# Emitting TensorE's work by the clock of a planner in the builder, in place of a fixed cycle of two steps

## The chip, the core and the metric

The kernel runs on one core of a Trainium2 chip. The metric is device time in microseconds (us). Matrix products run on TensorE (PE in the profile), exponentials on ScalarE (ACT), most copies out of PSUM on VectorE (DVE), a few small operations on GpSimd (POOL); SyncE (SP) issues the DMAs. Each engine executes its own instructions in the order in which the builder, a Python program, emitted them. An instruction that waits holds up all that stand behind it on its engine.

## The reference

Two layers of attention and MLP on 2048 rows of width 512, each with a layer norm ahead and a residual sum. The second pair uses the same weights as the first. 32 heads of width 16 share one key and one value head.

```python
q = (x @ wq).reshape(B, S, H, Dh)            # S = 2048, H = 32, Dh = 16
k = x @ wk
v = x @ wv
scores = jnp.einsum("bhqd,bkd->bhqk", q, k) * (Dh ** -0.5)
p = _softmax(scores, axis=-1)
o = jnp.einsum("bhqk,bkd->bhqd", p, v)       # then @ wo
...
h = jnp.maximum(jnp.einsum("bsd,df->bsf", x, w1), 0)   # Dff = 1792
h @ w2
...
x = x + _A_ref(_layernorm(x, axis=-1), A_wq, A_wk, A_wv, A_wo)
x = x + _B_ref(_layernorm(x, axis=-1), B_w1, B_w2)
x = x + _A_ref(_layernorm(x, axis=-1), A_wq, A_wk, A_wv, A_wo)
x = x + _B_ref(_layernorm(x, axis=-1), B_w1, B_w2)
```

## The kernel before

**Units and steps.** The attention of both layers is cut into 64 units: 2 layers, 4 blocks of 512 query rows, 8 units of four heads. A unit has 16 steps, one for each tile of 128 keys; that makes 1024 steps (`order`). In a step, `scores` (L707, L708) runs twice. Each time, two matmuls, one on each half of the array's rows, fill one PSUM tile of 128x1024 (`fst`; there are two, one for each half step), and ACT takes the exponential of it into half of the SBUF tile `fp` (three buffers). `front` emits the first half step and `back` the second. The text calls such a half step S. `values` (L713) is V: four matmuls of 32 columns side by side, which add the step's values to `facc`. That is one PSUM tile in all; at the end of a unit DVE copies it out (`keep`, L720) before the next unit may begin. A tile `fst` can be written again when its exponential is done, so the S after next waits for ACT.

**Dense work.** Projections, the output product, the MLP, transposes and layer norms of a block are written as Python generators (`start`, `late`, `chain`, `queries`, `keys`), which emit some instructions and then yield how many slots of PE these took. One slot is a unit of dense work, W. In `batch` (L97) two products share the array by rows: two matmuls of 64 rows make one W, and after a turn of mostly 12 W the halves swap. Between the turns DVE reads one element of each result (`fseen`, L125), and behind the second turn the results are taken out of PSUM: for the MLP by L578 and L579, for the sums into the residual by L497. There are three tiles `fmisc` for all that. Where a later step needs a result at once, `until` forces its generator to run to that point; the products are then not paired (L94) and ACT helps to empty PSUM.

**What each layer waits for.** A chain of a block (output product, MLP, in the first layer also the keys of the second, for one block its queries too) is about 390 to 466 W and is due some 130 steps later; `rate` spreads what is left of it over the steps up to its due time. Since the keys of the second layer need the chain of the last block of the first, a long run of forced dense work stands early in the second layer's steps (1398 to 1457 us).

**The order on PE.** `in_pairs` emits two steps at a time. Its cycle is S S, half a window of W, S, the other half, S, then the values of two steps, V V. A window has 6, 8 or 12 W (`FEW`, `MANY`, `MOST`), by how much dense work is due. If less than 6 is due, or after a yield that asks for a pause, it emits S S V S S V with no W. A window ends at a yield of the form `("lag", n)`.

```python
            front(i)
            back(i)
            w, pause = self.window(size / 2)
...
            front(i + 1)
...
                w, pause = self.window(size - w)
...
            back(i + 1)
            products(i - 1, i)
```

**The end of a unit.** `after(i)` follows the V of a step. At the last step of a unit it issues the copy of the sums to DRAM (L729). For each second unit it then calls, by step number, `unit_sums` one step later (a DMA reads the denominators back, `flsum`), `unit_inverse` three steps later (L746 to L748 on DVE, which wait for that DMA) and `unit_norm` six steps later (L760 to L762, which wait for `frinv`, another round trip through DRAM).

Of the kernel before, what the change touches and what calls it, by code (L numbers as in the profile page):

```python
# [31 lines left out]
FEW, MANY, MOST = 6.0, 8.0, 12.0  # L32
# [8 lines left out]
class _Net:  # L41
# [55 lines left out]
    def batch(self, *jobs, between=None):  # L97

        mm = self.nc.tensor.matmul
        if self.exact or self.solo or self.forced or len(jobs) == 1:  # L100
            for ops, empty, rest in jobs:
                ps = self.misc()
                yield from self.mm3(ps, ops)
                empty(ps)
                if between:
                    between()
                    between = None
                yield from rest()
            return
        ps = [self.misc(), self.misc()]  # L110
        n = len(jobs[0][0])
        for turn in range(2):
            for i in range(n):
                for h in range(2):
                    j = h ^ turn
                    a, b = jobs[j][0][i]
                    r = slice(64 * h, 64 * h + 64)
                    mm(ps[j], a[r], b[r], start=(turn == 0 and i == 0), stop=(turn == 1 and i == n - 1),  # L118
                       skip_group_check=True)
                if i < n - 1:  # L120
                    yield 1.0
            if not turn:

                for t in ps:
                    self.nc.vector.tensor_copy(self.wt("seen", [1, 1]), t[0:1, 0:1])  # L125
# [153 lines left out]
    def keys(self, L, b, to=None):  # L279
        nc = self.nc  # L280
        ps = self.misc()
# [8 lines left out]
        yield ("lag", 0)  # L290
# [31 lines left out]
    def queries(self, L, b, groups, to=None):  # L322
# [7 lines left out]
        yield ("lag", 0)  # L330
# [38 lines left out]
    def start(self):  # L369
# [22 lines left out]
        for t in range(KT):  # L392
# [9 lines left out]
            if t % 2:  # L402
                yield ("lag", 0)
# [9 lines left out]
            if t == 3:  # L413
                yield from self.queries(0, 0, [0])
                yield from self.keys(0, b, self.xt2)
            elif t % 4 == 3:
                yield ("lag", 0)
                yield from self.keys(0, b, self.ot2)
                yield from self.queries(0, 0, [b])
# [10 lines left out]
    def late(self, L, blocks):  # L430

        xs = self.residual(L, blocks[0])
        yield ("lag", 1)
        for b in blocks:
            todo = []
            for s in range(4):
                self.ln(xs[s], s, todo)
                if s % 2:
                    yield ("lag", 0)
# [4 lines left out]
            yield ("lag", 0)  # L444
# [73 lines left out]
    def chain(self, L, b):  # L518
# [63 lines left out]
        def up(f):  # L582
# [7 lines left out]
            else:  # L590
                split(f + 2, (0,))

                def between():
# [3 lines left out]
                                     lambda ps, g=g: hidden(g, ps), lambda: ()) for g in (f, f + 1)], between=between)  # L597
# [23 lines left out]
        ready = []  # L621
# [19 lines left out]
    def flip(self, todo):  # L641

        while todo:
            yield from self.transposed(*todo.pop(0))
            yield from self.transposed(*todo.pop(0))
            yield ("lag", 0)
# [121 lines left out]
    def advance(self):  # L768
# [7 lines left out]
        g[1] -= self.worth(w)  # L776
        return w

    def worth(self, w):
        return w if not isinstance(w, tuple) else w[2] if len(w) > 2 else 0.0  # L780
# [28 lines left out]

    def window(self, n):  # L810

        done = 0.0
        while done < n and self.gens:
            w = self.advance()
            done += self.worth(w)
            if isinstance(w, tuple):
                return done, w[1]
        return done, None
# [32 lines left out]
    def in_pairs(self, n, front, back, product, after):  # L851


        due, hold, size = 0.0, 0, None

        def products(*js):
            for j in js:
                product(j)
                after(j)

        front(0)
        back(0)
        for i in range(1, n - 1, 2):
            due = min(due + 2 * self.rate(i, due), 2 * MOST) if self.gens else 0.0
            if hold or not self.gens or due < FEW:
                hold = max(0, hold - 1)
                for j in (i, i + 1):
                    front(j)
                    back(j)
                    products(j - 1)  # L870
                continue
            if size is None:
                size = MOST if due > 2 * MANY else MANY if due > MANY - 1 else FEW
            front(i)
            back(i)
            w, pause = self.window(size / 2)
            due -= w
            if w < 1.0:
                products(i - 1)
                front(i + 1)  # L880
                back(i + 1)
                products(i)
                hold, size = pause or 0, None
                continue
            front(i + 1)
            if pause is None:
                w, pause = self.window(size - w)
                due -= w
            back(i + 1)
            products(i - 1, i)  # L890
            if pause is not None:
                hold, size = pause, None
        front(n - 1)
        back(n - 1)
        products(n - 2, n - 1)

    def run(self):
        self.normed, self.todo = (1, 3), []
        self.have, self.haveq = [0, 0], {(L, b): 0 for L in range(2) for b in range(NB)}
        self.gens, self.lag, self.left, later = [], 0, 0.0, {}  # L900
# [74 lines left out]
        else:  # L975
            self.in_pairs(n, front, back, product, after)
# [85 lines left out]
```

## Time and profile before

| | us |
|---|---|
| runs of the kernel | 2729.46, 2724.5, 2721.78 (median 2724.5) |
| time of the profiled execution | 2722.86 |
| its span | 2721.0 |
| PE busy | 2469.6 (91%) |
| ACT busy | 1985.5 (73%) |
| DVE busy | 726.5 (27%) |
| first value product, last | 41, 2606 |

The profile is of one execution. Its span runs from the first instruction to the last; the execution's own time is 1.9 longer. In a row of the timeline stand the start, the length, the engine, the line, what is written and read, the shape and the number of instructions; behind it, in brackets, the idle time ahead and what ended it. Matmuls overlap, and their ends are modelled: the price of one is read from the distance of the starts. V appears as 8 matmuls for a step, since each of its four is recorded twice. In a view of stretches, x gives the number of instructions in each.

### The profile page before, as it was taken

What the parts mean: (1) busy time and instruction counts of PE and PEld (TensorE: products, weight loads), DVE (VectorE), ACT (ScalarE), POOL (GpSimd) and SP (SyncE); (2) the same over time, 40 slices, a digit from 0 to 9 for tenths busy, and PEclk for the clock granted to TensorE, in tenths of its full rate; (3) what the DMA queues carried; (4) which work ended last, traced back from release to release, by engine and by line L of the source; (5) the groups of instructions that cost most, each with busy time, mean ns of one, the idle gap of its engine ahead of it and who ended that gap; (6) DMA issues with size and microseconds to landing.
All of it is one profiled execution on the core that took longest, in us unless ns stands there. A gap on an engine that the chain in (4) does not pass through costs nothing.

```text
span 2721.0 us, 44845 instructions
## 1 busy us (share of the span) xinstructions
PE 2469.6 (91%) x18981; PEld 805.8 (30%) x18981; DVE 726.5 (27%) x1560; ACT 1985.5 (73%) x2112; POOL 211.5 (8%) x291
## 2 busy tenths in 40 slices
PE   6798888999899999999798988999999999999979
PEld 2222222323233333333243222233323332333324
DVE  4532324323231123111333122221113111311132
ACT  5687886777677788888642988787888887887830
POOL 2221114310000000000000010000000000000000
PEclk8998998999999999999899999999999999999989
DMA  2112123211221102110221121211022110211022
GB/s 83 46 55 75 37 79 116 72 56 39 70 69 54 34 34 71 61 50 26 78 66 35 51 64 42 81 54 58 28 69 69 53 35 21 84 60 54 20 98 71
DMA packets 106309, 157.78 MB, mean 58 GB/s; under 512 B 19425, under 2 KB 39153, under 8 KB 106097
## 3 DMA queue, kind: packets, MB, share of 16 engines
q1 hardware_dynamic: 106096, 154.82, 17.4%
q8 instruction: 150, 2.46, 0.4%
q14 instruction: 63, 0.51, 0.1%
HBM read 108.86 MB, written 45.88 MB: 57 GB/s over the span
## 4 chain that ended last, share of the span: by engine, by line
PE 52%; ACT 20%; DMA 3%; DVE 3%; issue 3%; POOL 1%; SPq 1%; ACTq 0%; POOLq 0%; DVEq 0%
PE facc L713 23%; ACT fp L708 20%; PE fmisc L118 12%; PE fst L707 12%; PE fmisc L94 5%; DMA flsum<-fod 1%; DMA frinv<-frd 1%; DMA frd<-flsum 0%; DMA fod<-faccs 0%; DVE fbst L245 0%; SPq L360 0%; DVE fxt L497 0%; POOL fbmv L249 0%; DVE fxtl L269 0%; POOL fwraw L459 0%
## 5 line engine op out<-in xcount | busy, mean ns | idle before, releaser
L708 ACT ACTIVATE fp<-fst 128x1024 f32<-128x1024 f32 x2048 | 1941.9, 1028 | 527.9 <-PE fst L707 522.0
L713 PE MATMUL facc<-fp,fva 128*32 128x512 f32 x8192 | 1021.3, 606 | 4.6 <-DVE faccs L720 4.3
L707 PE MATMUL fst<-fqop,fkop 64*128 64x512 f16 x4096 | 738.6, 383 | 127.6 <-ACT fp L708 84.7
L707 PEld LDWEIGHTS <-fkop 64*128 64x128 f16 x4096 | 217.0, 94 | 915.2 <-issue 822.7
L713 PEld LDWEIGHTS facc<-fp,fva 128*32 128x32 f32 x8192 | 203.5, 109 | 469.4 <-issue 456.1
L118 PE MATMUL fmisc<-fxth,fw 64*128 64x512 f16 x1408 | 232.7, 379 | 15.0 <-DVE fseen L125 13.7
L118 PE MATMUL fmisc<-fw,fhh 64*128 64x512 f16 x1344 | 216.4, 377 | 7.5 <-DVE fseen L125 7.3
L497 DVE SCALAR_TENSOR_TENSOR fxt<-fmisc,fxt 128x512 f32<-128x512 f32 x156 | 103.2, 684 | 371.6 <-PE fmisc L118 326.7
L125 DVE COPY fseen<-fmisc 1x1 f32<-1x1 f32 x240 | 25.6, 142 | 535.8 <-PE fmisc L118 535.4
L248 POOL TENSOR_SCALAR fbmv<-fbmv 128x1 f32<-128x1 f32 x84 | 22.2, 265 | 1853.3 <-DVE fbmv L247 1851.9
L118 PEld LDWEIGHTS <-fw 64*128 64x128 f16 x2112 | 110.9, 94 | 119.9 <-issue 19.6
L118 PE MATMUL fmisc<-fxtl,fw 64*128 64x512 f16 x704 | 137.8, 378 | 0.0
L118 PE MATMUL fmisc<-fw,fhl 64*128 64x512 f16 x672 | 130.8, 376 | 0.0
L720 DVE COPY faccs<-facc 128x512 f32<-128x512 f32 x64 | 44.1, 690 | 256.9 <-PE facc L713 256.9
L578 DVE TENSOR_SCALAR fhh<-fmisc 128x512 f16<-128x512 f32 x86 | 58.9, 685 | 184.4 <-PE fmisc L118 184.2
L265 PE MATMUL fmisc<-fident,fxn 128*128 128x128 f32 x336 | 57.5, 311 | 49.4 <-DVE fxn L254 45.4
L579 DVE SCALAR_TENSOR_TENSOR fhl<-fmisc,fhh 128x512 f16<-128x512 f32 x112 | 77.3, 691 | 57.3 <-ACT fhh L576 54.3
L118 PEld LDWEIGHTS <-fhh 64*128 64x128 f16 x1344 | 70.4, 94 | 73.3 <-issue 12.9
L576 ACT ACTIVATE fhh<-fmisc 128x512 f16<-128x512 f32 x26 | 15.4, 597 | 96.0 <-PE fmisc L94 92.1
L94 PE MATMUL fmisc<-fw,fhh 128*128 128x512 f16 x224 | 66.6, 379 | 0.0
L265 PEld LDWEIGHTS fmisc<-fident,fxn 128*128 128x128 f32 x336 | 41.0, 156 | 70.5 <-DVE fxn L254 48.0
L94 PE MATMUL fmisc<-fxth,fw 128*128 128x512 f16 x192 | 59.7, 388 | 0.7 <-ACT fxth L87 0.7
(132 smaller groups left out, 1308.8 us busy)
## 6 DMA issues: line engine op xcount, KB each, us to landing
fw<-fwd SPq DMA_DIRECT2D x196, 256.0 KB
fod<-faccs SPq DMA_DIRECT2D x64, 256.0 KB
fqop<-fqd SPq DMA_DIRECT2D x128, 98.0 KB
fxt<-in_A_x_dram SPq DMA_DIRECT2D x44, 256.0 KB
fqd<-fqh SPq DMA_DIRECT2D x128, 64.0 KB
foraw<-fod SPq DMA_DIRECT2D x32, 256.0 KB
frinv<-frd SPq DMA_DIRECT2D x32, 256.0 KB
fwraw<-in_B_w_dram SPq DMA_DIRECT2D x28, 256.0 KB
```

The source lines that it names most:

```text
L94: self.nc.tensor.matmul(ps, a, b, start=(i == 0), stop=(i == n - 1))
L118: mm(ps[j], a[r], b[r], start=(turn == 0 and i == 0), stop=(turn == 1 and i == n - 1), skip_group_check=True)
L125: self.nc.vector.tensor_copy(self.wt("seen", [1, 1]), t[0:1, 0:1])
L248: nc.gpsimd.tensor_scalar(mv[:, 2:3], mv[:, 1:2], EPS, self.xs ** -2, op0=ADD, op1=MUL)
L265: nc.tensor.transpose(ps[:, c * P:(c + 1) * P], xn[:, c * P:(c + 1) * P], self.ident)
L497: self.nc.vector.scalar_tensor_tensor(xt, ps, 1.0 / factor, xt, op0=MUL, op1=ADD)
L578: nc.vector.tensor_scalar(hh, ps, 0.0, None, op0=MAX)
L579: nc.vector.scalar_tensor_tensor(hl, ps, 0.0, _f(hh), op0=MAX, op1=SUB)
L707: nc.tensor.matmul(st[:, hf], self.kop[U // 32][h, kt * P:(kt + 1) * P], q[h, pr, :], start=True, stop=True)
L708: nc.scalar.activation(p[:, 2 * pr:2 * pr + 2], st, AF.Exp, scale=self.up ** -2)
L713: self.nc.tensor.matmul(acc[32 * j:32 * j + 32], self.va[U // 32][:, kt], p[:, 2 * pr + hf], start=start, stop=stop, skip_group_check=True)
L720: self.nc.vector.tensor_copy(self.sums[U], acc)
```

## The change

`in_pairs` and `window` go, and `timed` takes their place. It keeps a clock of its own: `now` for PE and `act` for ACT. S, V, W and the exponential have fixed costs in it, so have the change from S or W to V (`ENTER`) and back (`LEAVE`), and the delays between the engines. Whenever PE is free by this clock, it picks the next piece: S if its PSUM tile is free by then, V if its exponentials are done, W if dense work is due and no pause is running. V waits until it fits, or until three steps' values stand together (the three buffers of `fp` set that limit). So the values of one to three steps follow each other. Each yield of the generators now also tells a pause, `free`, in the same clock: it is the time for which no further W is emitted, 0.5 to 3.6. The numbers of exponentials, products and DMAs are the same; 36 W are emitted unpaired that were paired.

```diff
-FEW, MANY, MOST = 6.0, 8.0, 12.0
+SCORE, VALUE, DENSE, EXP = 0.216, 0.858, 0.2155, 0.925
+TO_ACT, TO_PE, ENTER, LEAVE, COPY = 0.2, 0.22, 0.126, 0.116, 1.1
+PRESSED, FORCED, FULL = 6.0, 12.0, 14.0
...
-    def batch(self, *jobs, between=None):
+    def batch(self, *jobs, between=None, hold=1.0):
...
-                yield 1.0
+                yield ("lag", 0, 1.0, 0.5)
...
-        yield ("lag", 0, 1.0)
+        yield ("lag", 0, 1.0, hold)
...
-            yield from self.batch(*jobs[i:i + 2])
+            yield from self.batch(*jobs[i:i + 2], hold=1.6)
...
-                    yield ("lag", 0)
+                    yield ("lag", 1, 0.0, 3.6)
...
+        while len(done) < n:
+            k, j = len(exps), len(done)
+            step = k // 2
+            ready = exps[k - 2] + TO_PE if k > 1 else 0.0
+            if k == 2 * n or (step > 2 and j <= step - 3):
+                ready = 1e9
+            made = max(exps[2 * j + 1] + 0.1, sums) if 2 * j + 1 < k else 1e9
+            work = bool(self.gens) and due >= 1.0 and now >= free
+            gap = ready - now
+            if last == "product" and made <= now and due >= PRESSED:
+                kind = "product"
+            elif gap <= (LEAVE if last == "product" else 0.0) and not (work and due >= FORCED):
+                kind = "score"
+            elif made <= now + ENTER and gap >= 0.8 and not (work and due >= PRESSED and last != "product" and step - j < 2):
+                kind = "product"
+            elif work:
+                kind = "work"
+            elif made <= now + 0.2 and gap >= 0.6:
+                kind = "product"
+            else:
+                kind = "score" if ready < 1e9 else "product"
+            turn(kind)
...
+                act = max(act, now + TO_ACT, done[step - 3] + TO_ACT if step > 2 else 0.0) + EXP
+                exps.append(act)
+            elif kind == "work":
+                w = self.advance()
+                now += DENSE * self.worth(w)
+                due -= self.worth(w)
+                if isinstance(w, tuple):
+                    free = now + w[3]
+            else:
+                now = max(now, made if made < 1e9 else 0.0) + VALUE
+                product(j)
+                after(j)
+                done.append(now)
+                sums = now + COPY if j + 1 < n and self.first(j + 1) else 0.0
```

What moves shows first on PE in the second layer, around step 846. Before, the order there is a run of two V, then four score matmuls (`fst`, S S), then dense work (`fmisc`):

```order
L713 MATMUL facc<-fp,fva_78 32x512 x8
L707 LDWEIGHTS fkop_76
L707 MATMUL fst_20340<-fqop_91,fkop_76 128x512
L707 LDWEIGHTS fkop_76
L707 MATMUL fst_20340<-fqop_91,fkop_76 128x512
L707 LDWEIGHTS fkop_76
L707 MATMUL fst_20344<-fqop_91,fkop_76 128x512
L707 LDWEIGHTS fkop_76
L707 MATMUL fst_20344<-fqop_91,fkop_76 128x512
L118 LDWEIGHTS fhl
L118 MATMUL fmisc<-fw_19456,fhl 128x512
```

Now a single V (4 matmuls) stands there, one S behind it, and one or two W before the next S:

```order
L716 MATMUL facc<-fp,fva_78 32x512 x4
L710 LDWEIGHTS fkop_76
L710 MATMUL fst_20230<-fqop_90,fkop_76 128x512
L710 LDWEIGHTS fkop_76
L710 MATMUL fst_20230<-fqop_90,fkop_76 128x512
L122 LDWEIGHTS fw_19907
L122 MATMUL fmisc<-fxtl,fw_19907 128x512
L122 LDWEIGHTS fw_19903
L122 MATMUL fmisc<-fxtl,fw_19903 128x512
L710 LDWEIGHTS fkop_76
L710 MATMUL fst_20236<-fqop_90,fkop_76 128x512
L710 LDWEIGHTS fkop_76
```

V has moved between the two S of a step, and W with it. A little further in the changed order, where much dense work is due, stands a run of three V:

```order
L716 MATMUL facc<-fp,fva_78 32x512 x12
L710 LDWEIGHTS fkop_76
L710 MATMUL fst_20325<-fqop_91,fkop_76 128x512
L710 LDWEIGHTS fkop_76
L710 MATMUL fst_20325<-fqop_91,fkop_76 128x512
L710 LDWEIGHTS fkop_76
L710 MATMUL fst_20329<-fqop_91,fkop_76 128x512
L710 LDWEIGHTS fkop_76
L710 MATMUL fst_20329<-fqop_91,fkop_76 128x512
L122 LDWEIGHTS fhh
L122 MATMUL fmisc<-fw_19434,fhh 128x512
```

Behind it two S follow at once as before; the six W after them come without a break. In all, the order before has 627 runs of V (397 of two, 230 of one), the changed one 693 (501 of one, 53 of two, 139 of three).

On DVE the second place is the end of a unit in the second layer (unit 45). `faccs` is the copy of the unit's sums, `fgood` and the two rows after it are `unit_inverse`. Before:

```order
L720 COPY faccs<-facc 128x512
L125 COPY fseen<-fmisc 1x1 x2
L578 TENSOR_SCALAR fhh<-fmisc 128x512
L579 SCALAR_TENSOR_TENSOR fhl<-fmisc,fhh 128x512
L578 TENSOR_SCALAR fhh<-fmisc 128x512
L579 SCALAR_TENSOR_TENSOR fhl<-fmisc,fhh 128x512
L746 SCALAR_TENSOR_TENSOR fgood<-flsum,fgood 128x32 x2
L747 TENSOR_SCALAR flsum<-flsum 128x32
L748 RECIPROCAL flsum<-flsum 128x32
L760 TENSOR_TENSOR foraw<-foraw,frinv 128x512
```

And in the changed order:

```order
L723 COPY faccs<-facc 128x512
L129 COPY fseen<-fmisc 1x1 x2
L749 SCALAR_TENSOR_TENSOR fgood<-flsum,fgood 128x32 x2
L750 TENSOR_SCALAR flsum<-flsum 128x32
L751 RECIPROCAL flsum<-flsum 128x32
L763 TENSOR_TENSOR foraw<-foraw,frinv 128x512
L764 CAST foth<-foraw 128x512
L765 TENSOR_TENSOR fotl<-foraw,foth 128x512
```

The four evictions of an MLP batch (`fhh`, `fhl`) stood ahead of `fgood`; they now come later, and `fgood` follows the copy and one pair of `fseen`.

More of the change, by code (lines that the diff above doesn't have):

```diff
@@ L289, in keys @@
             eng.tensor_sub(kop[r:r + DH], kv[r:r + DH], _f(kop[r:r + DH]))
-        yield ("lag", 0)
+        yield ("lag", 0, 0.0, 1.2)
         ps = self.misc()
@@ L326, in queries @@
         for i in range(0, len(jobs), 2):
-            yield from self.batch(*jobs[i:i + 2])
+            yield from self.batch(*jobs[i:i + 2], hold=1.6)
         if self.exact:
             return
-        yield ("lag", 0)
+        yield ("lag", 1, 0.0, 2.4)
         ps = self.misc()
@@ L401, in start @@
             yield from self.transposed(xn[t], t % 4, self.ot2 if b else self.xt2)
-            if t % 2:
-                yield ("lag", 0)
+            yield ("lag", 0, 0.0, 2.4)
             if t == 1:
@@ L416, in start @@
             elif t % 4 == 3:
-                yield ("lag", 0)
+                yield ("lag", 0, 0.0, 1.6)
                 yield from self.keys(0, b, self.ot2)
@@ L432, in late @@
         xs = self.residual(L, blocks[0])
-        yield ("lag", 1)
+        yield ("lag", 1, 0.0, 2.0)
         for b in blocks:
@@ L438, in late @@
                 if s % 2:
-                    yield ("lag", 0)
+                    yield ("lag", 1, 0.0, 3.6)
                     yield from self.transposed(*todo.pop(0))
@@ L443, in late @@
                 xs = self.residual(L, b + 1)
-            yield ("lag", 0)
+            yield ("lag", 0, 0.0, 3.0)
             yield from self.queries(L, b, range(4))
@@ L596, in up @@
             yield from self.batch(*[(self.projection(w[0, g], slice(0, P), self.xt2),
-                                     lambda ps, g=g: hidden(g, ps), lambda: ()) for g in (f, f + 1)], between=between)
+                                     lambda ps, g=g: hidden(g, ps), lambda: ()) for g in (f, f + 1)], between=between, hold=1.6)
         def down(fs):
@@ L645, in flip @@
             yield from self.transposed(*todo.pop(0))
-            yield ("lag", 0)
+            yield ("lag", 1, 0.0, 3.2)
     def finish(self, L, b, s, xt, apart):
@@ L776, in advance @@
         g[1] -= self.worth(w)
+        self.spent += self.worth(w)
         return w
     def worth(self, w):
-        return w if not isinstance(w, tuple) else w[2] if len(w) > 2 else 0.0
+        return w[2] if isinstance(w, tuple) else w
     def until(self, done):
@@ L808, in pump @@
         return 0.0
[L810 to L818, printed above, removed]
     def order(self):
@@ L849, in alternate, with timed, turn @@
                     back(i + 1)
[L851 to L857, printed above, removed]
+    def timed(self, steps, front, back, product, after):
+        n = len(steps)
+        now = act = due = free = sums = 0.0
+        exps, done, last = [], [], None
+        def turn(kind):
+            nonlocal now, last
+            if (kind == "product") != (last == "product"):
+                now += ENTER if kind == "product" else LEAVE
+            last = kind
+        while len(done) < n:
[20 more added lines that the diff above has]
+            turn(kind)
+            if kind == "score":
+                now = max(now, ready) + SCORE
+                if k % 2 == 0:
+                    before = self.spent
+                    front(step)
+                    now += DENSE * (self.spent - before)
+                    due = min(due + self.rate(step, due), FULL) if self.gens else 0.0
+                else:
+                    back(step)
+                act = max(act, now + TO_ACT, done[step - 3] + TO_ACT if step > 2 else 0.0) + EXP
[6 more added lines that the diff above has]
+                    free = now + w[3]
+            else:
+                now = max(now, made if made < 1e9 else 0.0) + VALUE
@@ L858, in products @@
                 product(j)
                 after(j)
[L861 to L892, printed above, removed]
@@ L893, in in_pairs @@
-        front(n - 1)
-        back(n - 1)
-        products(n - 2, n - 1)
+                done.append(now)
+                sums = now + COPY if j + 1 < n and self.first(j + 1) else 0.0
     def run(self):
@@ L975, in run @@
         else:
-            self.in_pairs(n, front, back, product, after)
+            self.timed(steps, front, back, product, after)
         while not self.exact and self.gens:
```

2 lines of the change are left out of this document (1 added, 1 removed).

## The prediction

> **What bounds the kernel now.** I read the page first, then the budget by stretches, then one piece of the timeline on PE and ACT, and last the list of waits. The profiled execution took 2722.9 us by its own time, 1.9 more than its span, and lies 1.6 under the median of the three runs (2724.5); the sum below is made against 2722.9.
>
> ```profile
> span 2721.0 us, 44845 instructions
> PE 2469.6 (91%) x18981; PEld 805.8 (30%) x18981; DVE 726.5 (27%) x1560; ACT 1985.5 (73%) x2112; POOL 211.5 (8%) x291
> ```
>
> PE is busy for 91% of the span and ACT for 73%. Neither is full, and both are needed by each of the 1024 steps. A step has two pairs of score matmuls (S), two exponentials on ACT, and one value product (V). Between them stand units of dense work (W: one slot of the MLP or of a projection).
>
> ```profile
> L708 ACT ACTIVATE fp<-fst 128x1024 f32<-128x1024 f32 x2048 | 1941.9, 1028 | 527.9 <-PE fst L707 522.0
> L578 DVE TENSOR_SCALAR fhh<-fmisc 128x512 f16<-128x512 f32 x86 | 58.9, 685 | 184.4 <-PE fmisc L118 184.2
> L579 DVE SCALAR_TENSOR_TENSOR fhl<-fmisc,fhh 128x512 f16<-128x512 f32 x112 | 77.3, 691 | 57.3 <-ACT fhh L576 54.3
> L265 PE MATMUL fmisc<-fident,fxn 128*128 128x128 f32 x336 | 57.5, 311 | 49.4 <-DVE fxn L254 45.4
> ```
>
> The 2048 exponentials alone fill 1941.9 us. The idle time on ACT ahead of them is put down to PE:
>
> ```profile
> ACT fp L708 <- PE fst L707: 522.0, 465, 7.7
> ```
>
> So ACT waits for PE to issue scores. Does PE have that much work, or does it wait too? Over four stretches between the first value product (41 us) and the last (2606 us), the exponentials give the steps (x divided by 2):
>
> ```profile
> core 0: us, ACT busy (x), PEclk, DMA share, GB/s
> 41.00:368.00 327.00, 244.28 (x257) 0.97 0.16 49
> 368.00:1305.00 937.00, 718.48 (x759) 0.99 0.18 59
> 1305.00:1710.00 405.00, 252.73 (x266) 0.97 0.18 57
> 1710.00:2606.00 896.00, 722.34 (x766) 1.00 0.16 53
> ```
>
> The paired dense matmuls of the same stretches (two to a unit), and the unpaired ones (one to a unit):
>
> ```profile
> 41.00:368.00 327.00, 36.62 (x288) 15.22 (x288) 0.97 0.16 49
> 368.00:1305.00 937.00, 315.76 (x2376) 125.16 (x2376) 0.99 0.18 59
> 1305.00:1710.00 405.00, 64.32 (x492) 26.08 (x492) 0.97 0.18 57
> 1710.00:2606.00 896.00, 302.84 (x2316) 121.50 (x2316) 1.00 0.16 53
> ```
>
> ```profile
> 41.00:368.00 327.00, 17.59 (x72) 6.31 (x72) 0.97 0.16 49
> 368.00:1305.00 937.00, 5.87 (x24) 2.02 (x24) 0.99 0.18 59
> 1305.00:1710.00 405.00, 72.62 (x312) 31.39 (x312) 0.97 0.18 57
> ```
>
> That is 128.5, 379.5, 133 and 383 steps, with 216, 1212, 558 and 1158 units. Prices come from two pieces of the timeline on PE. In the first a step has no dense work. The two S of the step stand at 900.44 and 901.35:
>
> ```profile
> 899.41 1.06 PE L713 MATMUL facc<-fp,fva 128*32 128x512 f32 x8
> 900.44 0.39 PE L707 MATMUL fst<-fqop,fkop 64*128 64x512 f16 x2
> 901.35 0.39 PE L707 MATMUL fst<-fqop,fkop 64*128 64x512 f16 x2 [0.52 <-ACT fp L708]
> 901.67 1.07 PE L713 MATMUL facc<-fp,fva 128*32 128x512 f32 x8
> 902.67 0.91 PE L707 MATMUL fst<-fqop,fkop 64*128 64x512 f16 x4
> ```
>
> A lone V takes 1.00 us from its start until the next S (901.67 to 902.67). The second S starts 0.91 after the first, though two S need only 0.22 each (below): it waited for the exponential that frees its PSUM tile. From V to V this step took 2.26 us. In the second piece two V stand together, and the work between them is S S W4 S W4 S:
>
> ```profile
> 905.66 1.92 PE L713 MATMUL facc<-fp,fva 128*32 128x512 f32 x16
> 907.52 0.61 PE L707 MATMUL fst<-fqop,fkop 64*128 64x512 f16 x4
> 907.96 0.38 PE L118 MATMUL fmisc<-fw,fhl 64*128 64x512 f16 x2
> 908.18 0.59 PE L118 MATMUL fmisc<-fw,fhh 64*128 64x512 f16 x4
> 908.61 0.38 PE L118 MATMUL fmisc<-fw,fhl 64*128 64x512 f16 x2
> 909.09 0.39 PE L707 MATMUL fst<-fqop,fkop 64*128 64x512 f16 x2
> ...
> 910.17 0.39 PE L707 MATMUL fst<-fqop,fkop 64*128 64x512 f16 x2
> 910.49 1.92 PE L713 MATMUL facc<-fp,fva 128*32 128x512 f32 x16
> ```
>
> Two V take 1.86 from start to the next S, so a further V costs 0.86. From the last S to V passes 0.32 where S takes 0.22 (907.52 to 907.96 for two). A run of V thus costs 0.86 for each V and 0.24 for entering and leaving (0.10 + 0.14). The cycle is 4.83 us for two steps and eight units. Its work is 4 x 0.22 + 2 x 0.86 + 0.24 + 8 x 0.216 = 4.57, so PE waited about 0.26 to 0.28, most of it ahead of the S at 909.09. The 0.216 of a unit is from the longest stretch of nothing but dense work in the chain of waits:
>
> ```profile
> 1398.41 58.40 PE fmisc L94 x270
> ```
>
> For ACT in the same cycle:
>
> ```profile
> 908.01 3.77 ACT L708 ACTIVATE fp<-fst 128x1024 f32<-128x1024 f32 x4 [1.08 <-PE fst L707]
> ```
>
> Four exponentials take 3.77 us. One lasts 1.03 (page) and they start 0.91 apart, so a step needs 1.82 us of ACT. An exponential starts 0.49 after its S (907.52 to 908.01), and 1.08 after its start the S that reuses the tile may go (908.01 to 909.09). These four numbers price any order of S, V and W.
>
> PE's work in the four stretches, by steps x (0.44 + 0.86), units x 0.216 and runs x 0.24 (94, 211, 98 and 223 runs of V in the order before) is 236, 806, 317 and 802 us, 2161 together. Transposes add about 35 (the row of L265 has 57.5 us in all, a part of it ahead of the first step or after the last). The stretches last 2565. **PE therefore stands still for about 370 us**, and that, not its work, is what another order can change. ACT's own floor, 1024 x 1.82 = 1864, is lower than PE's 2196.
>
> **The change part by part.** The work is the same. By the order, dense units keep their number apart from 36 which change from paired to unpaired at equal price; tiles, buffers and DMAs stay. What changes is which of S, V and W stands next.
>
> *Runs of V.* Before there are 627 (397 of two, 230 of one), now 693 (501 of one, 53 of two, 139 of three): 66 more x 0.24 = +16 us. The Trainium skill ("TensorEngine Tiling (Array Packing)", Key Properties) says that changing the tiling mode, not just the tile, drains the TensorE, which speaks against more runs. The trace shows a price of that kind, the 0.24, and the sum goes by it. If each of the two changes cost the fixed part of a matmul's latency that the Trainium skill gives ("TensorE: Matmul & The Clock Gate", Single matmul latency: about 166 ns), it would be 22, an estimate from that page.
>
> *Waits for ACT that go.* Before, 265 cycles of two steps with work wait 0.28 each (74 us), 141 lone steps without work 0.72 (101), 67 lone steps with work about 0.28 (901.67 to 905.66 against 3.71 of work; 19): 194 us.
>
> *Waits for ACT that come.* The commonest piece of the new order is V S W2 S, 221 times: 0.86 + 0.24 + 0.44 + 0.43 = 1.97 us, over ACT's 1.82. With S at 0 and V behind it, the next S comes at 1.32 and the reuse of the first tile at 1.97, free since 0.49 + 1.08 = 1.57: no wait. V S W S (95 times) has 1.76 of work and waits 0.06 for ACT, V S S (73) waits 0.28: together 26 us. After a run of three (2.82 us) ACT has run dry. S S W6 S W3 S W3 S fits again: third S at 1.74 (free 1.57), fourth at 2.6 (free 0.49 + 0.91 + 1.08 = 2.48). Of 192 runs of two or three, 65 go on with W6 like this. About 100 have fewer units or a second S at once: S S W5 S S has its fourth S at 1.79 and waits 0.69, S S W1 S waits 0.91, S S W1 S S 1.6. By their counts the mean is 0.75: 75 us. Sum 101 in place of 194.
>
> *Waits for results.* The other 370 - 194 = 176 us before is PE standing at dense work, transposes and products whose inputs aren't there, as in the first stretch (327 us for 250 of work). New pauses after each yield (0.5 to 3.6 in the planner's clock) let PE pass on to S or V instead. No row of before shows such a pause. At best two thirds go (58 stay); at worst none by this count (176), or more (rivals). I take the middle of 176 and two thirds of it, 146, nearer to the worst, since many of them come from DVE:
>
> ```profile
> DVE fgood L746 <- DMA flsum<-fod: 109.7, 20, 11.6
> DVE foraw L760 <- DMA frinv<-frd: 117.3, 27, 7.0
> ```
>
> DVE stands still for 227 us at the head of its queue, for a DMA which the order doesn't make faster; evictions of dense work queue behind it. In the new order the reciprocal follows closer on its request at some unit pairs, where all three V of a run call their follow-ups at once: at 8 of 31 pairs nothing but one V (0.86) lies between, where before it was most of a cycle of 4.83, some 3.4 with the V. It parks DVE about 2.6 us more there, 21 in all, but the S S W that follow the run need no new eviction; I cost it at nothing, and the full 21 lie within the range.
>
> Sum: 16 + 101 + 146 = 263 against 370, so -107: **2722.9 - 107 = 2616 us**, 3.9% less.
>
> **The rivals.** (a) *Dense work arrives before its evictions are done.* A batch (24 units, 2736 / 24 = 114 of them paired) ends with up to four evictions on DVE, 4 x 0.69 = 2.76 us (rows L578, L579). Before, a run of two and two S (1.96 + 0.44 = 2.4) cover most of it. Now the planner's pause there is 1.0 to 1.6. If PE stands for the missing 1.16 at each, and for the 21 above, it is 114 x 1.16 + 21 = 153 more: 2769, slower. It decides from 0.94 us per batch on. For it: PE is in order. Against: three PSUM tiles serve two in use, only the first tile's evictions are needed, and before shows little of such waits:
>
> ```profile
> PE fmisc L118 <- DVE fseen L125: 27.2, 22, 5.3
> ```
>
> (b) *The waits only move.* The planner's clock runs off the chip's, S waits as often as before, and just the 66 extra runs are paid: 2723 + 16 = 2739, slower. Against it: its constants (0.216, 0.858, 0.126 + 0.116, 0.925) are within 0.02 of the rows above.
>
> (c) *Runs of three starve ACT more than I count.* If each of the 100 waits 1.6, it is 85 more: 2701.
>
> (d) *The pauses work.* Only 58 of the 176 stay: 2722.9 - 370 + 16 + 101 + 58 = 2528.
>
> (e) *The order isn't what is said.* Refuted by the counts of runs.
>
> **How the numbers follow.** The forecast with its neighbourhood (2570 to 2680) has 0.60, (d) 0.12, (c) 0.10, (b) 0.08, (a) 0.06, and 0.04 that gains and losses cancel within 0.3%, about what a measurement of this kernel tells from no change. Faster: 0.60 + 0.12 + 0.10 = 0.82; same 0.04; slower 0.14. The range leaves out the far half of (d) at the bottom, and (a), (b) and what cancels at the top: 2550 to 2710.
>
> **What would show it.** In the stretches with most dense work (1710 to 2606 before, 383 steps in 896 us, 2.34 a step) I expect 2.22 to 2.28 a step; in the early one (327 us for 128.5 steps) about 295. The pieces V S W2 S must take near 1.97, a run of three 2.82 from the S before it. The waits of dense matmuls for DVE should stay below 60 us in the list. Wrong would be: dense matmuls waiting for DVE by over 100 us (a); S waiting for ACT as now (b), with the idle time ahead of the exponentials still over 500 us; it should fall to about 420.

## The result and the profile after

The changed kernel takes 2703.2 us (median of 6 runs, 2698.11 to 2708.0). The kernel before, on the same chip, takes 2728.03 (6 runs, 2721.78 to 2732.29). The ratio is 0.9911 with an interval of 0.9894 to 0.9929: faster by 0.9%, some 25 us. The forecast was 107 us. The profiled execution of the changed kernel took 2704.14 us, against 2722.86 before. Of all the runs below, one stands apart and is left out: keep_act took 4716.36 us once in four runs, for a reason that isn't known.

The head of its page, the row of the exponentials and the row of V:

```profile
span 2702.3 us, 44789 instructions
PE 2449.1 (91%) x18945; PEld 825.2 (31%) x18945; DVE 723.0 (27%) x1554; ACT 1992.3 (74%) x2114; POOL 211.9 (8%) x291
L711 ACT ACTIVATE fp<-fst 128x1024 f32<-128x1024 f32 x2048 | 1947.5, 1028 | 488.4 <-PE fst L710 470.3
L716 PE MATMUL facc<-fp,fva 128*32 128x512 f32 x8192 | 1039.6, 609 | 54.7 <-DVE faccs L723 37.0
```

The idle time ahead of the exponentials fell from 527.9 to 488.4, not to 420. The new thing is in the last row: 54.7 us in which PE stood ahead of V, 37.0 of them for the copy of the sums on DVE. Here is the same row before:

```profile
L713 PE MATMUL facc<-fp,fva 128*32 128x512 f32 x8192 | 1021.3, 606 | 4.6 <-DVE faccs L720 4.3
```

In the list of waits (total, times, longest) of the changed kernel stand with it:

```profile
DVE fgood L749 <- DMA flsum<-fod: 173.9, 27, 14.9
...
PE facc L716 <- DVE faccs L723: 37.0, 15, 12.1
...
PE fmisc L122 <- DVE fseen L129: 21.1, 10, 7.6
...
PE facc L716 <- DVE fseen L129: 14.0, 2, 11.0
...
PE fmisc L122 <- DVE fhl L582: 8.8, 5, 2.8
```

DVE's wait for the denominators grew from 109.7 to 173.9 us, and a single wait of V for DVE reached 12.1. Of the 14.0 us in which V stood for `fseen`, 11.0 are one wait, taken up with the experiments. Dense products wait little for DVE (21.1 + 8.8).

The exponentials over the same four parts of the program:

```profile
core 0: us, ACT busy (x), PEclk, DMA share, GB/s
40.00:366.00 326.00, 239.45 (x251) 0.93 0.16 49
366.00:1300.00 934.00, 731.12 (x770) 0.98 0.18 60
1300.00:1695.00 395.00, 244.62 (x258) 0.94 0.18 58
1695.00:2586.00 891.00, 728.88 (x770) 0.99 0.17 54
```

The last stretch has 385 steps in 891 us, 2.31 a step, where 2.22 to 2.28 was forecast and 2.34 stood before. The first has 125.5 steps in 326 us: nothing gained there, where 30 us was forecast.

**Where V waits.** PE in the changed kernel, at the end of a unit of the first layer:

```profile
224.52 1.06 PE L716 MATMUL facc<-fp,fva 128*32 128x512 f32 x8
225.52 0.39 PE L710 MATMUL fst<-fqop,fkop 64*128 64x512 f16 x2
226.11 0.39 PE L710 MATMUL fst<-fqop,fkop 64*128 64x512 f16 x2 [0.20 <-ACT fp L711]
238.58 1.93 PE L716 MATMUL facc<-fp,fva 128*32 128x512 f32 x8 [12.07 <-DVE faccs L723]
```

And DVE at that time (brackets: idle time ahead and what ended it):

```profile
214.97 0.69 DVE L357 TENSOR_TENSOR fql<-fmisc,fqh 128x512 f16<-128x512 f32 x1
225.71 0.69 DVE L454 BATCH_NORM_STATS2 fbst<-fwraw 128x6 f32<-128x512 f32 x1 [10.05 <-DMA fwraw<-in_A_wo_dram]
...
228.02 0.43 DVE L463 CAST fwoh<-fwraw 128x512 f16<-128x512 f32 x1 [1.40 <-POOL fwraw L462]
228.36 0.67 DVE L341 TENSOR_SCALAR fqr<-fmisc 32x512 f16<-32x512 f32 x1
234.50 0.69 DVE L249 BATCH_NORM_STATS2 fbst<-fxt 128x6 f32<-128x512 f32 x1 [5.47 <-DMA fxt<-in_A_x_dram]
...
237.84 0.68 DVE L723 COPY faccs<-facc 128x512 f32<-128x512 f32 x1
```

DVE first stands 10.05 us for a piece of the output weight, then 5.47 us for the residual rows. Only behind both stands the copy at 237.84, though the V at 224.52 was the unit's last. The next V needs that copy, because `facc` is one PSUM tile. PE is in order, so the S behind that V stands too, and with it ACT. The budget by stretches, here of all engines, shows PE and ACT nearly empty for 12.5 us (PE, PEld, DVE, ACT, POOL), and the granted clock at 0.61:

```profile
226.00:238.50 12.50, 0.39 (x2) 0.09 (x1) 4.91 (x11) 1.89 (x3) 4.23 (x6) 0.61 0.25 87
```

The kernel before has the same stop on DVE, at the same place of its program:

```profile
209.86 0.69 DVE L451 BATCH_NORM_STATS2 fbst<-fwraw 128x6 f32<-128x512 f32 x1 [10.07 <-DMA fwraw<-in_A_wo_dram]
...
212.17 0.43 DVE L460 CAST fwoh<-fwraw 128x512 f16<-128x512 f32 x1 [1.40 <-POOL fwraw L459]
212.51 0.68 DVE L720 COPY faccs<-facc 128x512 f32<-128x512 f32 x1
```

There the stop ended when PE had just come to the end of the unit. PE went on without a gap (DVE's next stop, 11.41 us for the denominators, then cost it 4.93 at a transpose, at 228.54):

```profile
212.41 0.88 PE L707 MATMUL fst<-fqop,fkop 64*128 64x512 f16 x4
213.25 1.92 PE L713 MATMUL facc<-fp,fva 128*32 128x512 f32 x16
```

So the stop isn't new. What is new is that PE stands behind it: in the changed order the copy has come to lie behind both stops, where before it stood ahead of the residual's. The Trainium skill ("TensorE: Matmul & The Clock Gate", Architectural detail) says that VectorE's queue is strictly first in, first out; these rows agree, with 12.07 us as the price.

### The profile page after: what moved, and what is told of

Its sections match the earlier page's. It is cut to its first block, busy times and chain, and to the rows that moved or that the text cites. A ratio compares the mean times of both kernels' runs of the same rounds, so it can differ in the third digit from the quotient of the medians.

```text
span 2702.3 us, 44789 instructions
## 1 busy us (share of the span) xinstructions
PE 2449.1 (91%) x18945; PEld 825.2 (31%) x18945; DVE 723.0 (27%) x1554; ACT 1992.3 (74%) x2114; POOL 211.9 (8%) x291
## 4 chain that ended last, share of the span: by engine, by line
PE 56%; ACT 10%; DMA 5%; DVE 5%; issue 2%; SPq 1%; POOL 1%; ACTq 0%; POOLq 0%; DVEq 0%
PE facc L716 24%; PE fmisc L122 14%; PE fst L710 12%; ACT fp L711 10%; PE fmisc L98 6%; DMA flsum<-fod 2%; DMA fod<-faccs 1%; DMA frinv<-frd 1%; DVE fbst L249 1%; DVE fxt L500 1%; PE fmisc L269 0%; DVE faccs L723 0%; SPq L364 0%; DMA frd<-flsum 0%; DVE fhh L581 0%
## 5 line engine op out<-in xcount | busy, mean ns | idle before, releaser
L711 ACT ACTIVATE fp<-fst 128x1024 f32<-128x1024 f32 x2048 | 1947.5, 1028 | 488.4 <-PE fst L710 470.3
L716 PE MATMUL facc<-fp,fva 128*32 128x512 f32 x8192 | 1039.6, 609 | 54.7 <-DVE faccs L723 37.0
L710 PE MATMUL fst<-fqop,fkop 64*128 64x512 f16 x4096 | 776.4, 384 | 90.0 <-ACT fp L711 75.0
L710 PEld LDWEIGHTS <-fkop 64*128 64x128 f16 x4096 | 247.9, 94 | 898.6 <-issue 766.1
L122 PE MATMUL fmisc<-fxth,fw 64*128 64x512 f16 x1376 | 242.5, 380 | 21.5 <-DVE fseen L129 12.5
L249 DVE BATCH_NORM_STATS2 fbst<-fxt 128x6 f32<-128x512 f32 x84 | 57.7, 687 | 21.4 <-DMA fxt<-in_A_x_dram 11.8
```

What stands on the lines that cost most here:

```text
L249: nc.vector.bn_stats(st, xt)
L710: nc.tensor.matmul(st[:, hf], self.kop[U // 32][h, kt * P:(kt + 1) * P], q[h, pr, :], start=True, stop=True)
L711: nc.scalar.activation(p[:, 2 * pr:2 * pr + 2], st, AF.Exp, scale=self.up ** -2)
L716: self.nc.tensor.matmul(acc[32 * j:32 * j + 32], self.va[U // 32][:, kt], p[:, 2 * pr + hf], start=start, stop=stop, skip_group_check=True)
```

## The waiting of PE, sorted

I worked out PE's waiting inside the 1024 steps from the starts of its matmuls: the distance of two starts, less the price of the first (S or W 0.2155; V 0.883, or 0.974 where no V follows; entering V 0.107; a group of four transposes 0.44). A wait of an S under 2.2 us counts as a wait for ACT. Of the others, one beside an idle stretch of DVE that a DMA ended counts for that, one beside an idle stretch that POOL ended counts for POOL. This is a sorting by neighbourhood, so single entries may be off by some us, and a sum by some 10 with other prices (more in no_pauses, whose sum is the least certain). Remainders under 0.05 us stand in the sum only. Matmuls that run slower at a lower clock count as waits here too.

| kernel (profiled run) | for ACT | DVE stopped by a DMA | DVE stopped by POOL | other | sum |
|---|---|---|---|---|---|
| before | 231 | 50 | 11 | 85 | 378 |
| after | 149 | 93.5 | 20 | 82 | 346.5 |
| before_late | 229 | 12 | 19 | 89 | 349 |
| after_late | 166 | 31 | 26 | 80 | 305 |
| before_loads | 231 | 49 | 11 | 86 | 378 |
| after_loads | 158 | 86 | 20 | 70 | 337 |
| before_all | 230 | 12 | 17 | 88 | 347 |
| after_all | 171 | 4 | 23 | 71 | 272 |
| all_two | 162 | 16 | 22 | 66 | 271 |
| all_pauses | 201 | 18 | 18 | 76 | 313 |
| keep_act | 153 | 95 | 16 | 66 | 334 |
| no_pauses | 97 | 142 | 35 | 222 | 504 |
| all_scale | 172 | 4 | 5 | 80 | 264 |

From before to after the sum falls by 31.5. The 66 runs of V more cost 66 x (0.107 + 0.091) = 13 by these prices. That leaves 18.5, against the 18.7 between the two profiled executions. The waits for ACT fell by 82; those at DVE's stops rose by 52 (43.5 and 9).

## The experiments

The theory was that DVE, stopped at the head of its queue by a DMA, holds the copy of the sums, and with it V, PE and ACT (A in the expectations). The rivals put the shortfall elsewhere: in the pauses and the price of the extra runs (B), in the lower granted clock as a cause of its own (C), in evictions that wait in place of V (D), or in the starving of ACT after runs of three (S). The edits to loads, denominators and scaling were also made to the kernel before, as controls; the other four have none. Ratios are to the kernel before on the same chip. Differences in us are of medians, some of them from different chips; on those the kernel before took 2725.5 to 2728.4.

### The loads earlier: after_loads, before_loads

The output weight is loaded six steps ahead of its split, and the generator pauses longer between the load of the residual and its first use. In the kernel before, the pause became `("lag", 2)`. These are two edits in one, and the second isn't the same in both kernels; they were not tried apart.

```diff
-        self.parts(self.wo2[0][:, c], self.wo2[1][:, c], raw, 2, c)
+        self.woraw = raw
+    def split_wo(self, c):
+        self.parts(self.wo2[0][:, c], self.wo2[1][:, c], self.woraw, 2, c)
...
-        yield ("lag", 1, 0.0, 2.0)
+        yield ("lag", 1, 0.0, 9.0)
...
-            at(36 + 8 * c, self.load_wo, c)
+            at(30 + 8 * c, self.load_wo, c)
+            at(36 + 8 * c, self.split_wo, c)
```

> The changed kernel, with the four loads of wo issued six steps ahead of the DVE work on them, and a pause of 9.0 in place of 2.0 behind the residual loads of the late projections. Theory A (the lost gain is V waiting for the copy of facc, which stands on DVE behind an instruction that waits for a DMA): the V waits of 12.1 us at 226 and 5.8 at 1554 go, PE's waits fall by 20 to 30, about 2678 (from 2703). Theory B (the gain is lost in the planner's pauses and in the price of the extra runs, not on DVE): within 8 of 2703. Theory C (the lower granted clock, 0.966 for 0.978, is a cause by itself): clock stays 0.966, time within 8.

> The kernel before with the same earlier loads of wo, and a yield of two pairs in place of one behind the residual loads. Theory A: there the waits for these loads stand at transposes and cost less: gains 5 to 15, 2713 to 2723 (from 2728). Theory B: within 5 of 2728.

Measured: after_loads 2689.58 us, ratio 0.9863 [0.9846, 0.9879], 14 below the changed kernel. before_loads 2723.82 (10 runs), 0.9995 [0.9986, 1.0005]: nothing, where 5 to 15 had been expected. The first lies between the two theories, the second is a miss. The edit is worth nothing to the kernel before, and some 14 to the changed one. C expected the clock to stay at 0.966 and the time within 8 of 2703: the clock rose to 0.970 (median of the runs) with the 14. How much of any gain here comes by way of the clock isn't separated.

### The denominators later: after_late, before_late

`unit_inverse` moves from three steps behind the request to six, `unit_norm` and `follow` from six to ten, but for the last unit of a layer.

```diff
-                    at(i + 3, self.unit_inverse, U)
-                    at(i + 6, self.unit_norm, U)
+                    far = U not in (31, 63)
+                    at(i + (6 if far else 3), self.unit_inverse, U)
+                    at(i + (10 if far else 6), self.unit_norm, U)
...
-                        at(i + 6, follow, U // 32, (U // 8) % 4)
+                        at(i + (10 if far else 6), follow, U // 32, (U // 8) % 4)
```

> The changed kernel with the reciprocal of a unit pair six steps behind its end in place of three, and its normalisation ten in place of six (except at units 31 and 63). Theory A: the wait of fgood for flsum falls from 174 us to under 60 and that of foraw for frinv to under 60, PE's waits near them (67 us, of which some 55 inside the steps) fall by 20 to 40: about 2675. Theory B: DVE's wait goes and the time stays within 8 of 2703.

> The kernel before with the same later reciprocal and normalisation. Theory A: its waits near such stops are 43 us inside the steps, and it gains 10 to 25 (2703 to 2718). Theory B: within 5 of 2728.

Measured: after_late 2667.51, 0.9788 [0.9772, 0.9805], 36 below the changed kernel. before_late 2694.63, 0.9882 [0.9866, 0.9899], 31 below the kernel before, more than the 10 to 25 expected. DVE's wait went, and the longest wait of V stayed:

```profile
DVE fgood L749 <- DMA flsum<-fod: 42.8, 10, 10.2
...
PE facc L716 <- DVE faccs L723: 33.0, 11, 12.2
```

What this stop did in the changed kernel stands in its rows on DVE, at 566 to 582 us:

```profile
565.76 0.69 DVE L582 SCALAR_TENSOR_TENSOR fhl<-fmisc,fhh 128x512 f16<-128x512 f32 x1
573.54 0.42 DVE L749 SCALAR_TENSOR_TENSOR fgood<-flsum,fgood 128x32 f32<-128x32 f32 x2 [7.09 <-DMA flsum<-fod]
...
579.85 0.69 DVE L763 TENSOR_TENSOR foraw<-foraw,frinv 128x512 f32<-128x512 f32 x1 [5.29 <-DMA frinv<-frd]
...
581.65 0.20 DVE L129 COPY fseen<-fmisc 1x1 f32<-1x1 f32 x2
```

and on PE:

```profile
573.67 0.61 PE L710 MATMUL fst<-fqop,fkop 64*128 64x512 f16 x4
581.90 1.04 PE L122 MATMUL fmisc<-fw,fhh 64*128 64x512 f16 x4 [7.62 <-DVE fseen L129]
```

Two round trips to DRAM follow each other at the head of DVE. PE issued its turn of 12 W behind them and stands 7.62 us for a copy of one element. Both kernels pay for such places, so this edit alone doesn't explain why the change gained so little.

### Both: after_all, before_all

> The changed kernel with both: the later reciprocal and the earlier loads. Theory A (DVE waiting for a DMA at the head of its queue holds up the copy of facc and the evictions): the two gains add up, 36 + 14 = 50, about 2653. Rival: they overlap, 2662 or more.

> The kernel before with both. Theory A: 31 + 2, about 2693. If the change's shortfall is DVE's waiting alone, the two with both edits stand some 75 or more apart; if they stand apart by only 40 (2653 to 2693), most of the shortfall is elsewhere.

Measured: after_all 2631.05, 0.9651 [0.9632, 0.9671], 72 below the changed kernel, more than 36 and 14 together. before_all 2693.74, 0.9882 [0.9862, 0.9902], 32 below the kernel before on its chip, no better than before_late. **With both edits the change is worth 2693.74 - 2631.05 = 63 us, 2.3%; without them 25, 0.9%.** That lies between the 75 and the 40 of the expectation. With the later denominators alone it is worth 2694.63 - 2667.51 = 27: on top of them the loads are worth 36 to the changed kernel and 1 to the kernel before. The waits of after_all, to be read against those of the changed kernel (lines are 3 higher):

```profile
DVE fgood L752 <- DMA flsum<-fod: 48.7, 13, 10.9
...
PE facc L719 <- DVE faccs L726: 8.0, 6, 3.0
```

V's wait for the copy is 8.0 us in place of 37.0. The steps, timed in the profiled executions from the starts of V, tell where the edits work:

| steps | before | before_all | after | after_loads | after_late | after_all |
|---|---|---|---|---|---|---|
| 1 to 32 | 97.5 | 97.3 | 112.7 | 99.8 | 106.4 | 99.6 |
| 32 to 128 | 227.4 | 216.2 | 219.5 | 214.5 | 220.0 | 201.3 |
| 128 to 505 | 934.3 | 917.7 | 916.4 | 918.0 | 903.7 | 901.9 |
| 505 to 640 | 408.3 | 409.3 | 410.4 | 408.9 | 404.1 | 396.7 |
| 640 to 1024 | 898.3 | 894.3 | 888.2 | 895.0 | 868.0 | 867.8 |

In steps 32 to 128, with the output weight, the residual loads and the denominators all there, the edits alone give 5.0 and -0.5, together 18.2. One stop of DVE lies in the shadow of another: with the loads earlier, DVE stands 10.20 us for the denominators at 218.15. In steps 640 to 1024, with no weight to load, the later denominators alone give the changed kernel 20.2, and both edits give the kernel before 4.0. In these executions the worth of the change rises by 50 with the edits (18.7 to 68.9): by 16 in steps 640 to 1024, 15 in steps 505 to 640, 13 in steps 1 to 32 and 7 in steps 32 to 128, with -2 in steps 128 to 505. No single stretch holds most of it, and not all of the 13 in steps 1 to 32 comes from the edits (see what stays open).

DVE can also hold V without a stop by a DMA. The first row is the changed kernel, the second before_all:

```profile
420.88 3.64 PE L716 MATMUL facc<-fp,fva 128*32 128x512 f32 x16 [10.96 <-DVE fseen L129]
```

```profile
405.87 3.29 PE L716 MATMUL facc<-fp,fva 128*32 128x512 f32 x16 [12.61 <-DVE faccs L723]
```

Both times DVE was splitting four pieces of a weight for some 12 us, 7.1 of them waiting for POOL, with the copy behind. In the kernel before the same splits cost PE 5.3, and in after_all 8.1, at dense products. The edits thus moved the control's V behind these splits, and some 10 us of what the change is worth with the edits come from these places and not from stops by a DMA (12.6 for 5.3 in the control, 8.1 for 11.0 in the changed kernel).

### The copy of the sums on ACT: keep_act

In the changed kernel, ACT copies out the sums in place of DVE.

```diff
-            self.nc.vector.tensor_copy(self.sums[U], acc)
+            if self.exact:
+                self.nc.vector.tensor_copy(self.sums[U], acc)
+            else:
+                self.nc.scalar.activation(self.sums[U], acc, AF.Copy)
```

> The changed kernel, with the first copy of facc out of PSUM (64 times) on ACT in place of DVE, so that V no longer stands behind DVE's queue; ACT gets 64 x 0.6 = 38 us more. Theory A: V's waits for faccs (37 us on PE in the list) fall under 10, and the time by 15 to 30 from 2703. Rival D (what V doesn't wait, the evictions wait): within 8 of 2703.

Measured: 2681.94 (median of three runs), 0.9836 [0.981, 0.9862], 21 below the changed kernel, as A expected and more than rival D. V hardly waits for the copy any more, but the dense work waits longer for DVE than in the changed kernel (21.1 and 8.8 there):

```profile
PE fmisc L122 <- DVE fseen L129: 32.3, 13, 9.8
...
PE fmisc L122 <- DVE fhl L582: 18.5, 5, 11.1
...
PEld facc L716 <- ACT faccs L726: 13.1, 31, 0.8
```

The stops of DVE cost PE 95 us by the sorting, as before the edit (93.5); the sorting shows the gain under "other" (82 to 66). By stretches it lies where the longest wait was: steps 32 to 128 took 209.2 in place of 219.5, while steps 640 to 1024 took 892.0 in place of 888.2. So the place of the copy is a part of the price, and elsewhere whatever PE needs next from DVE waits. Moving the copy does less than moving the stops.

### No pauses: no_pauses

In the changed kernel, no pause is kept after a yield.

```diff
-                    free = now + w[3]
+                    free = now
```

> The changed kernel without the planner's pauses behind a yield. If the pauses keep PE from standing at work whose inputs aren't there: 30 or more slower than 2703. If they cost more than they keep away: faster by 10 or more.

Measured: 2889.67, 1.0602 [1.058, 1.0625], 187 above the changed kernel. Dense work runs into its evictions, as the forecast's rival (a) put it:

```profile
PE fmisc L269 <- DVE fxn L258: 81.3, 24, 13.9
...
PE fmisc L122 <- DVE fhl L582: 68.5, 38, 10.5
PE fmisc L122 <- DVE fseen L129: 67.8, 91, 4.8
```

The pauses do keep dense work from its evictions. They don't know of DVE's waits for DMAs.

### Longer pauses: all_pauses

On after_all, every pause is a quarter longer (`free = now + 1.25 * w[3]`).

> The changed kernel with the later reciprocal and the earlier loads (2631), and all the planner's pauses 1.25 times as long. If the pauses are still too short for what DVE needs: 10 or more faster. If they are long enough, dense work comes later and more of it is forced: 5 to 20 slower.

Measured: 2661.68, 0.9763 [0.974, 0.9786], 31 above after_all, more than the 5 to 20 expected. The waits for ACT rise from 171 to 201. Dense work that is put off comes back: 828 W are forced and unpaired, against 804.

### Two V as soon as two stand: all_two

On after_all, a run begins when two steps' values stand, so that runs of three all but vanish (696 runs in all).

```diff
+            elif step - j >= 2 and k % 2 == 1 and made <= now + ENTER and last != "product":
+                kind = "product"
```

> The changed kernel with the later reciprocal and the earlier loads (2631), and V emitted as soon as two steps' values stand: runs of one and two, almost none of three (696 runs in place of 667). Theory S (runs of three leave ACT dry, and S waits behind them, 157 x 0.5 to 0.75): S's waits fall by 40 or more, the runs cost 29 x 0.24 = 7, so 20 to 40 faster. Rival (the dry ACT costs PE little, as S S W6 S W3 S W3 S shows): within 10 of 2631.

Measured: 2626.88, 0.9627 [0.9609, 0.9645], 4 below after_all, with intervals that overlap, where 20 to 40 was expected if runs of three starve ACT. The waits for ACT fall by 9 (171 to 162). So runs of three are not what starves ACT most in after_all; on the changed kernel itself this wasn't tried.

### The scaling on DVE: all_scale, before_scale

On both kernels with both edits, the scaling of a weight moves from POOL to DVE, so that DVE needn't wait for POOL in the middle of a split.

```diff
-            nc.gpsimd.tensor_scalar(raw, raw, self.ws, None, op0=MUL)
+            nc.vector.tensor_scalar(raw, raw, self.ws, None, op0=MUL)
```

> The changed kernel with the later reciprocal and the earlier loads (2631), and the scaling of the raw weights on DVE in place of POOL (32 times 0.7 us on DVE, where it waited for POOL 1.4 to 1.9). Theory A, in its wider form (DVE waiting for anything at the head of its queue holds up V and dense work): the 23 us of PE's waits near DVE's waits for POOL fall by 8 to 15, about 2619. Rival (DVE's added work costs as much): within 5 of 2631.

> The kernel before with the later reciprocal, the earlier loads and the scaling on DVE: the control for the 2613 of the changed kernel with the same three. If DVE's waits were what ate the change's gain, the kernel before gains less from this edit (0 to 10 below its 2694, as PE stood 17 us near DVE's waits for POOL there), and the two stand 70 to 85 apart, against 25 without the edits. If the edits serve both alike, it falls to about 2676 and the distance stays at 63.

Measured: all_scale 2613.28, 0.9579 [0.9559, 0.9599], 18 below after_all and the fastest version found. before_scale 2678.94, 0.9825 [0.9807, 0.9844], 15 below before_all, more than the 0 to 10 expected there if DVE's waits for POOL had eaten the change's gain. The edit serves both alike, so these waits are no part of the shortfall. By the sorting they fall from 23 to 5 and from 17 (before_all) to 1.

With all three edits on either kernel the change is worth 2678.94 - 2613.28 = 66 us.

## Why the prediction was right in sign and wrong in size

**Right: the prices of the pieces.** PE in the changed kernel, V S W2 S three times and then a run of three (the rows left out are of the same kind):

```profile
1852.31 1.07 PE L716 MATMUL facc<-fp,fva 128*32 128x512 f32 x8
1853.31 0.39 PE L710 MATMUL fst<-fqop,fkop 64*128 64x512 f16 x2
...
1853.97 0.38 PE L710 MATMUL fst<-fqop,fkop 64*128 64x512 f16 x2
1854.28 1.07 PE L716 MATMUL facc<-fp,fva 128*32 128x512 f32 x8
...
1857.90 0.38 PE L710 MATMUL fst<-fqop,fkop 64*128 64x512 f16 x2
1858.21 2.78 PE L716 MATMUL facc<-fp,fva 128*32 128x512 f32 x24
1860.92 0.60 PE L710 MATMUL fst<-fqop,fkop 64*128 64x512 f16 x4
```

From V to V 1.97 us (1852.31 to 1854.28), as forecast; from the S at 1857.90 to the next 3.02, less 0.22 for the S itself 2.80, where 2.82 was forecast. A run of V costs 0.20 to enter and leave by the medians, 13 us for 66, where 16 was forecast.

**Near in its difference, and partly by luck: the waits for ACT.** Forecast from 194 to 101, -93; sorted from the traces from 231 to 149, -82. Both ends were too low by 37 and 48: the pieces counted are the common ones, and the waits outside them were not priced. With the stops moved, the fall is only 59 (below), so the stops helped to bring the 82 near.

**Wrong: the step "waits for results", 176 to 146, and in it the sentence that the parking of DVE costs nothing.** These waits rose from 147 to 197 (the sum less those for ACT), by 50, where they were to fall by 30. That is 80 of the 88 us by which the profiled executions miss the forecast (107 against 18.7); the waits for ACT account for 11 more, the runs give 3 back. The forecast saw that DVE stands 227 us at the head of its queue, and asked which evictions of dense work queue behind it. It didn't ask what else does: the copy of `facc`, the only PSUM tile of V. And it counted just the denominators among the stops, though the two loads make V's longest wait. The longer parking of DVE, put at 21 us at most and costed at nothing, came out as 64 more for the denominators (109.7 to 173.9). Taken as constant, the stops seemed no part of the change. But a stop's price depends on what PE needs next from DVE at that moment. In the fixed cycle a stop of 10.07 us cost V nothing at 213; in the new order one of 10.05 and one of 5.47 cost 12.07 at 226.

**What the runs showed in its place.** With these stops moved the change is worth 63 to 66 us, as the controls on both kernels show, against 25 with the stops where they were; some 10 of that difference come from the weight splits ahead of 405.87 and 420.88. That is still 41 to 44 short of 107. By the sorting, from before_all to after_all the waits for ACT fall by 59 and not 93, and all others by 16 together and not 30, while 38 more runs of V (629 to 667) cost 7.5. So the term that is left too large is the fall of the waits for ACT. These waits are higher in after_all (171) than in the changed kernel (149). While PE stands for DVE, ACT empties the tiles; take that away, and part of the gain comes back as waits for ACT. That reading fits the rows; no run shows it by itself.

**The rivals.** (a) is what comes without the pauses (2889.67), and not with them. (b), that waits for ACT only move, falls with the 82 us. (c), the runs of three, falls with all_two as far as that run reaches; its 2701 lies close to the 2703 measured by chance, as its mechanism isn't what the runs show. (d) doesn't show. The measured time lies at the upper end of the range for a reason that no rival named.

**What stays open.** Steps 1 to 32 took 112.7 us in the changed kernel, 97.5 before and 99.6 in after_all. A part is a stop again: behind the wait for the residual's rows, a V at 145.98 stands 3.67 us for the sums on DVE, and the four steps around it take 17.6 us, in after_all 10.8. Another part is no matter of the order. after_late has the same order on PE up to 379 us, and took 106.4. The first row is the changed kernel, the second after_late, over the same two steps:

```profile
81.70:104.60 22.90, 16.70 (x66) 4.50 (x58) 7.04 (x16) 6.89 (x8) 6.70 (x8) 0.70 0.00 1
```

```profile
78.00:97.60 19.60, 13.41 (x70) 4.19 (x64) 7.20 (x16) 7.04 (x8) 6.77 (x8) 0.91 0.00 1
```

The clock was granted at 0.70 and 0.91 there. Why it differs between two executions with the same order on PE isn't known. That the edit to the loads is worth nothing to the kernel before is read from where its stops lie, as at 210; a kernel before with the stop moved to another place wasn't tried.

## What to carry to other kernels

A planner that keeps the clocks of two engines needs also the third one's queue: ask of every instruction that waits for a DMA what stands behind it on its engine, and who needs that next. Put such an instruction later than the longest round trip in the trace, or load earlier, before judging a new order; and make the same edit to the old order too, since only the difference shows what it hid. Waits that overlap hide one another: two edits that give 14 and 36 alone gave 72 together, so a small gain by one alone doesn't clear the other.

## What the runs showed of the hardware

- A stop of DVE can begin before its DMA is even issued. These are the issues on SP in the changed kernel for two of the stops above, the weight's load and the denominators' request:

```profile
221.05 0.62 SPq L242 DMA_DIRECT2D fwraw<-in_A_wo_dram  x1
```

```profile
568.22 0.57 SPq L741 DMA_DIRECT2D flsum<-fod  x1
```

  DVE began to wait for the weight at 215.66 (225.71 less 10.05), 5.4 us ahead of the issue, and went on 4.7 behind it. For the denominators it began at 566.45 and went on 5.3 us behind the issue. SP's rows from 213.64 to 221.05 follow each other almost without a break, each a transfer of another tile. So half of the stop for the weight is SP's queue of earlier transfers.
- The granted clock of TensorE is lower where PE stands longer for DVE's stops by DMAs: 0.985 in after_all (4 us of them by the sorting), 0.978 before (50), 0.966 after (93.5), 0.954 in no_pauses (142), and 0.61 in the 12.5 us around the longest wait. The first V after that wait took 1.93 us in its row, where one elsewhere takes 1.06. The Trainium skill ("TensorE: Matmul & The Clock Gate", What's actually happening) says that the clock falls to half after an idle window of about 3.4 us. The 0.61 over a stretch with 0.39 us of PE's work fits that. So a long wait is paid for a second time behind its end, as in that row.
